# Pairs of PSUM banks as single tiles, in a fused attention and highway kernel

## The chip, the cores and the metric

The kernel runs on one core of a Trainium2 chip. The metric is device time in microseconds (us) of one launch; lower is better. The profile is one execution, and its span runs from the first to the last instruction, about 1.8 us less than the device time.

The granted TensorE clock (1.0 is full speed) differs between executions. Single runs of one kernel differ by 1 to 2 us. All ratios and verdicts below use the runs that were classed as fast. The medians in the tables are of all runs: those of e1, e3, e11 and e12 each contain one run classed as slow.

## The reference

Inputs are q, k and v of shape (8, 8, 576, 64), two 512x512 weights and a bias.

```python
q_s = exp(q - max(q, -1));  q_s /= sum(q_s, -1)          # over the 64 columns
k_s = exp(k - max(k, 2));   k_s /= sum(k_s, 2)           # over the 576 tokens
kv  = einsum('bhsd,bhse->bhde', k_s, v)                  # 64x64 per head
x   = einsum('bhsd,bhde->bhse', q_s, kv)  ->  (4608, 512)
H = relu(x @ w_h);  T = sigmoid(x @ w_t + b_t)
out = T * H + (1 - T) * x
```

## The kernel before

There are eight rounds of attention, b = 0 to 7, one per batch. Each exponentiates q and k, transposes q on TensorE (`q_trans`, three groups of transposes, profile name `pq`), forms the kv products (`kv_half`, `psk`), divides them by the sums that a column of ones has gathered (`kv_norm`), and multiplies out x (`x_pair`, `px`, for eight of nine token blocks; `x_left`, `px_l`, for the ninth). Beside round b + 1 run the dense products of chunk c = b: gate (`pt`) and carry (`ph`), then `nat` tiles that turn the result back for output. The program is emitted in a hand-made order of "slots", eight per round, and each engine gets its part in that order; TensorE's list from 9.81 to 22.11 us keeps it, group by group. The program holds eight banks of PSUM; before the change four serve gate and carry, three rotate for attention, one turns results back.

```python
    ps_ht = pool("ps_ht", 4, space=PSUM)
    ps_q = pool("ps_q", 3, space=PSUM)
    ps_nat = pool("ps_nat", 1, space=PSUM)
    # ... cut ...
    def warm_mid(n):                       # matmuls on zeros
        t = ps_q.tile([P, 512], FP32, tag="qx", name="warm_mid")
        for _ in range(n):
            mm(t, ident, wide, True, True)
    # ... cut ...
    def kv_norm(b):
        rz = small.tile([P, 2, 2], FP32, tag="rz", name=f"rz_{b}")
        for x in range(2):
            nc.vector.reciprocal(rz[:, x], psk[b][x][:, :, 64])
        for x in range(2):
            nc.vector.tensor_mul(kvn[b % 2][:, x], psk[b][x][:, :, 0:64],
                                 rz[:, x].broadcast_to([P, 2, 64]))
    # ... cut ...
    def x_pair(b, a, even=False, home=None):
        # ... cut: two one-bank tiles t[0], t[1]; four 64x64 matmuls of 512 columns ...
        for c in range(2):
            dst = xT[g][:, 2 * a + c, :, b2, :]
            if (c == 0) if even else (b > 2 or a + c < 2):
                nc.scalar.copy(dst, t[c])
            else:
                nc.vector.tensor_copy(dst, t[c])
```

The softmax here doesn't subtract the row's maximum and nothing guards it: scores larger than these inputs give would overflow.

Of the kernel before, what the change touches and what calls it, by code (L numbers as in the profile page):

```python
# [9 lines left out]
FP32 = mybir.dt.float32  # L10
FP16 = mybir.dt.float16
# [3 lines left out]
PSUM = bass.MemoryType.PSUM  # L15
# [3 lines left out]
def kernel(  # L19
# [10 lines left out]
    nc = tc.nc  # L30
    B, H, S, D = q.shape
    P = 128
    PAD = 128
    N9 = S // 64
    NM = N9 - 1
# [4 lines left out]
    def heads_view(t, b):  # L40
        return t[b].rearrange("(c x) (p n) d -> (x p) c (n d)", x=2, n=N9)

    pool = lambda name, bufs, **kw: ctx.enter_context(tc.tile_pool(name=name, bufs=bufs, **kw))
# [10 lines left out]
    gp = pool("gp", 2)  # L54
    mo = pool("mo", 3)
    ps_ht = pool("ps_ht", 4, space=PSUM)
    ps_q = pool("ps_q", 3, space=PSUM)
    ps_nat = pool("ps_nat", 1, space=PSUM)

    ctx.enter_context(tc.manual_schedule())  # L60
# [2 lines left out]
        o, l, r, start=st, stop=sp, skip_group_check=True  # L63
# [90 lines left out]
        for _ in range(n):  # L154
            mm(warm, ident, wide, True, True)

    def warm_mid(n):
        t = ps_q.tile([P, 512], FP32, tag="qx", name="warm_mid")
        for _ in range(n):
            mm(t, ident, wide, True, True)  # L160


    ek, eq, psk, qsT = {}, {}, {}, {}
# [28 lines left out]

    def kv_half(b, a):
        if a == 0:
            psk[b] = [
                ps_q.tile([P, 2, 256], FP32, tag="qx", name=f"psk_{b}_{x}")
                for x in range(2)
            ]
        for n in range(N9):
            for c in range(2):  # L200
                for x in range(2):
                    r = slice(64 * x, 64 * x + 64)
                    mm(
                        psk[b][x][64 * c : 64 * c + 64, a, 0:65],
                        ek[b][r, n, 2 * a + c, :], v16s[b % 2][r, n, 2 * a + c, 0:65],
                        n == 0, n == N9 - 1,
                    )

    def kv_norm(b):
        rz = small.tile([P, 2, 2], FP32, tag="rz", name=f"rz_{b}")  # L210
        for x in range(2):
            nc.vector.reciprocal(rz[:, x], psk[b][x][:, :, 64])
        for x in range(2):
            nc.vector.tensor_mul(
                kvn[b % 2][:, x], psk[b][x][:, :, 0:64],
                rz[:, x].broadcast_to([P, 2, 64]),
            )

    qsum = {}

# [33 lines left out]
        e, r = eq[b][:, n0:n1], qsum[b][:, n0:n1]  # L254
        nc.gpsimd.tensor_mul(e, e, r.broadcast_to(list(e.shape)))  # L255

    def q_trans(b, g, eng=None):
        if g == 0:
            qsT[b] = qtp.tile([P, 4, N9, 64], FP16, tag="qsT", name=f"qsT_{b}")
        n0, n1 = NG[g]  # L260
        w = n1 - n0
        t = ps_q.tile([P, 4, 4, 64], FP16, tag="qx", name=f"pq_{b}_{g}")
        for n in range(n0, n1):
            for a in range(2):
                ptrans(
                    t[:, 2 * a : 2 * a + 2, n - n0, :],
                    eq[b][:, n, 2 * a : 2 * a + 2, :].rearrange("p c d -> p (c d)"),
                )
        if eng is nc.scalar:
            nc.scalar.copy(qsT[b][:, :, n0:n1, :], t[:, :, 0:w, :])  # L270
        else:
            nc.vector.tensor_copy(qsT[b][:, :, n0:n1, :], t[:, :, 0:w, :])  # L272

    def x_pair(b, a, even=False, home=None):
        ps, tag = home or (ps_q, "qx")
        g, b2 = b // 2, b % 2
        if a == 0 and b2 == 0:
            xT[g] = xtp.tile([P, 4, NM, 2, 64], FP16, tag="xT", name=f"xT_{g}")
        t = [
            ps.tile([P, NM, 64], FP32, tag=tag, name=f"px_{b}_{a}_{c}")  # L280
            for c in range(2)
        ]
        for x in range(2):
            for c in range(2):
                r = slice(64 * c, 64 * c + 64)
                mm(
                    t[c][64 * x : 64 * x + 64].rearrange("p n d -> p (n d)"),
                    kvn[b % 2][r, x, a, :],
                    qsT[b][r, 2 * a + x, 0:NM, :].rearrange("p n d -> p (n d)"),
                    True, True,  # L290
                )
        for c in range(2):
            dst = xT[g][:, 2 * a + c, :, b2, :]
            if (c == 0) if even else (b > 2 or a + c < 2):
                nc.scalar.copy(dst, t[c])  # L295
            else:
                nc.vector.tensor_copy(dst, t[c])

    def x_left(b):
        for c in range(2):  # L300
            t = ps_q.tile([P, 2, 64], FP32, tag="qx", name=f"px_{b}_l{c}")
            r = slice(64 * c, 64 * c + 64)
            for a in range(2):
                for x in range(2):
                    mm(
                        t[64 * x : 64 * x + 64, a, :], kvn[b % 2][r, x, a, :],
                        qsT[b][r, 2 * a + x, NM, :], True, True,
                    )
            x9v = x9.rearrange("p (a c) b d -> p a c b d", c=2)
            nc.vector.tensor_copy(x9v[:, :, c, b, :], t)  # L310


    rows_of = lambda c: 8 if c < B else 4
# [9 lines left out]

    live = {}

    def gate(c, ob, home=None):
        xv = views(c)[0]
        ps, tag = home or (ps_ht, "ht")
        ps = ps.tile([P, rows_of(c), 64], FP32, tag=tag, name=f"pt_{c}_{ob}")
        for k_ in range(4):  # L330
            mm(ps, w16["t"][:, k_, ob * P : ob * P + P], xv(k_), k_ == 0, k_ == 3)
        nc.scalar.activation(ps, ps, AF.Tanh, bias=bt2[:, ob : ob + 1], scale=0.5)  # L332
        live[c, ob] = ps
# [36 lines left out]
    o32 = {}  # L370
# [11 lines left out]
    def out_tile(g, n, spare=False):  # L382
        if n % 4 == 0:
            o32[g, n // 4] = og.tile([P, 4, 512], FP32, tag="o32", name=f"o32_{g}_{n}")
        ps, tag = (ps_q, "qx") if spare and n % 4 < 3 else (ps_nat, "nat")
        t = ps.tile([P, 4, P], FP32, tag=tag, name=f"nat_{g}_{n}")
        for k_ in range(4):
            turn_block(
                t, k_,
                None if k_ in added(g) else xT[g][:, k_, n].rearrange("p b d -> p (b d)"),  # L390
                gT[g][:, k_, n].rearrange("p b d -> p (b d)"),
            )
        o = o32[g, n // 4][:, n % 4, :]
        if spare and n % 2:
            nc.vector.tensor_copy(o, flat(t))
        else:
            nc.scalar.copy(o, flat(t))  # L397
        if n % 4 == 3:
            i = n // 4
            nc.sync.dma_start(rows[g][:, 4 * i : 4 * i + 4, :], o32[g, i])  # L400
# [8 lines left out]
    def tile9(g, nk):  # L409
        if g % 2 == 0:  # L410
            o32["9", g // 2] = og.tile([P, 4, 512], FP32, tag="o32", name=f"o9_{g}")
        t = ps_q.tile([P, 4, P], FP32, tag="qx", name=f"nat9_{g}")
        for k_ in range(nk):
            turn_block(t, k_, blk9(x9, g, k_), blk9(g9, g, k_))
        o = o32["9", g // 2][:, g % 2, 0 : nk * P]
        if g % 2:
            nc.vector.tensor_copy(o, flat(t)[:, 0 : nk * P])
        else:
            nc.scalar.copy(o, flat(t)[:, 0 : nk * P])
        if g % 2:  # L420
            nc.sync.dma_start(
                rows9[:, g - 1 : g + 1, 0 : nk * P],
                o32["9", g // 2][:, 0:2, 0 : nk * P],
            )
# [13 lines left out]
    def at(p, *fs):  # L438
        events.setdefault(p, []).extend(fs)
# [37 lines left out]
    for b in range(2, B):  # L477
        p = 8 * (b - 1)
        if b > 2:
# [11 lines left out]
            at(s + 0.9, E(cast_v, b, 1))  # L491
            at(s + 1, E(exp_half, b, "k", 1))
        tr, kv, x = {
            2: ((5, 6, 6.4), (4, 6.2), (7, 7.5, 7.6)),
            3: ((4, 5, 5), (3, 4), (6, 7, 7)),
            4: ((2, 3, 4), (4, 5), (6, 7, 7)),
        }.get(b, ((2, 3, 4), (3, 4), (5, 6, 7)))
        for i in range(3):
            at(p + tr[i], E(q_trans, b, i))
        at(p + kv[0], E(kv_half, b, 0))  # L500
        at(p + kv[1], E(kv_half, b, 1), E(kv_norm, b))
        at(p + x[0], E(x_pair, b, 0))
        at(p + x[1], E(x_pair, b, 1))
        at(p + x[2], E(x_left, b))
    for b in range(4, B):
        at(8 * (b - 3), *[E(load, b, w) for w in "qkv"])

    for f in [
# [3 lines left out]
        E(q_recip, 0), E(q_scale_v, 0, 0, 4), E(q_scale_v, 0, 4, N9),  # L512
        E(exp_half, 0, "k", 0), E(cast_v, 0, 0),
        E(exp_half, 0, "k", 1), E(cast_v, 0, 1),
        E(q_trans, 0, 0), E(q_trans, 0, 1), E(warm_up, 2), E(q_trans, 0, 2),
        E(warm_up, 6),
        E(kv_half, 0, 0), E(gate_bias), E(warm_up, 2), E(kv_half, 0, 1), E(kv_norm, 0),
        *[E(cast_weight, "t", k_, (nc.vector, nc.gpsimd)[k_ % 2]) for k_ in range(4)],
        E(warm_up, 4),
        E(x_pair, 0, 0), E(warm_up, 2), E(x_pair, 0, 1), E(warm_up, 1), E(x_left, 0),  # L520
        E(exp_half, 1, "q", 0), E(q_sums_tree, 1, 0),
        E(exp_half, 1, "q", 1), E(q_sums_tree, 1, 1), E(q_recip, 1),
        *[f for k_ in range(4) for f in (E(less_one, k_), E(cast_weight, "h", k_, nc.scalar, 0.5))],
        E(q_scale_p, 1, 0, 4), E(q_scale_p, 1, 4, 8),
        E(gate, 0, 0), E(gate, 0, 1), E(gate, 0, 2, (ps_q, "qx")), E(warm_mid, 5),
        E(carry, 0, 0), E(blend, 0, 0), E(carry, 0, 1), E(exp_half, 1, "k", 0),
        E(gate, 0, 3, (ps_nat, "nat")), E(blend, 0, 1), E(carry, 0, 2),
        E(q_trans, 1, 0), E(blend, 0, 2), E(carry_products, 0, 3),
        E(exp_half, 1, "k", 1),
        *[E(cast_v_head, 1, c, (nc.scalar, nc.gpsimd, nc.gpsimd, nc.scalar)[c]) for c in range(4)],  # L530
# [2 lines left out]
        *[E(load, 3, w) for w in "qkv"],  # L533
        E(q_trans, 1, 1), E(kv_half, 1, 0), E(kv_half, 1, 1), E(kv_norm, 1),
        E(q_trans, 1, 2), E(carry_diff, 0, 3), E(exp_half, 2, "q", 0),
        E(x_pair, 1, 0, True), E(x_pair, 1, 1, True, (ps_ht, "ht")),
        E(q_sums_tree, 2, 0), E(exp_half, 2, "q", 1), E(q_sums_tree, 2, 1), E(q_recip, 2),
    ]:
        f()
# [33 lines left out]
```

## Time and profile before

| | before |
|---|---|
| device time, median of the first three runs | 132.56 us (132.47 to 132.88) |
| span of the profiled run | 130.5 us, mean clock 0.996 |
| TensorE busy | 115.9 us (89 %) |
| VectorE busy | 101.0 us, 204 instructions |
| ScalarE busy | 93.0 us, 140 instructions |

Two views carry the argument: the table of busy time by windows, and the list of instructions in order of time, with start, duration, engine, line, operation and count, and the idle time before an instruction and what ended it in square brackets. The prediction below shows and reads both.

### The profile page before, as it was taken

What the parts mean: (1) busy time and instruction counts of PE and PEld (TensorE: products, weight loads), DVE (VectorE), ACT (ScalarE), POOL (GpSimd) and SP (SyncE); (2) the same over time, 40 slices, a digit from 0 to 9 for tenths busy, and PEclk for the clock granted to TensorE, in tenths of its full rate; (3) what the DMA queues carried; (4) which work ended last, traced back from release to release, by engine and by line L of the source; (5) the groups of instructions that cost most, each with busy time, mean ns of one, the idle gap of its engine ahead of it and who ended that gap; (6) DMA issues with size and microseconds to landing.
All of it is one profiled execution on the core that took longest, in us unless ns stands there. A gap on an engine that the chain in (4) does not pass through costs nothing.

```text
span 130.5 us, 3496 instructions
## 1 busy us (share of the span) xinstructions
PE 115.9 (89%) x1427; PEld 65.4 (50%) x1427; DVE 101.0 (77%) x204; ACT 93.0 (71%) x140; POOL 69.8 (53%) x64
## 2 busy tenths in 40 slices
PE   4969998996998799789998999989998999999960
PEld 1325442362444246536644654565466445589940
DVE  1397546898999997996996789987986756689870
ACT  3552049997988589669979969968992674666530
POOL 2005506690399999459919970996299523510000
PEclk9999999999999999999999999999999999999998
DMA  4999999999999999998999989990034006037874
GB/s 130 365 384 396 402 400 412 410 413 413 402 412 402 410 413 410 404 411 353 321 379 409 368 285 407 407 403 15 0 158 171 0 5 294 28 161 316 362 290 165
DMA packets 15848, 40.07 MB, mean 307 GB/s; under 512 B 724, under 2 KB 1240, under 8 KB 14808
## 3 DMA queue, kind: packets, MB, share of 16 engines
q1 hardware_dynamic: 15832, 39.85, 79.1%
q8 instruction: 11, 0.18, 0.5%
q14 instruction: 5, 0.04, 0.1%
HBM read 30.41 MB, written 9.44 MB: 305 GB/s over the span
## 4 chain that ended last, share of the span: by engine, by line
PE 43%; DVE 21%; DMA 11%; ACT 8%; issue 6%; POOL 5%; SPq 3%; DVEq 0%; POOLq 0%; ACTq 0%
PE pt L62 14%; PE ph L62 13%; DMA q<-in_q_dram 11%; PE nat L62 6%; DVE r L225 5%; DVE dd L350 4%; PE psk L62 4%; POOL eq L255 3%; PE pq L67 3%; DVE g L358 3%; PE px L62 2%; DVE qsT L272 2%; SPq L94 2%; ACT xT L295 2%; POOL v L182 2%
## 5 line engine op out<-in xcount | busy, mean ns | idle before, releaser
L255 POOL TENSOR_TENSOR eq<-eq,r 128x1024 f16<-128x1024 f16 (+2 forms) x16 | 29.7, 1874 | 15.9 <-DVE r L243 15.9
L332 ACT ACTIVATE pt<-pt,bt 128x512 f32<-128x512 f32 (+1 forms) x40 | 24.8, 624 | 14.1 <-PE pt L62 14.1
L62 PE MATMUL ph<-xT,w16h 128*128 128x512 f16 x128 | 33.3, 380 | 0.8 <-ACT w16h L114 0.4
L62 PE MATMUL pt<-xT,w16t 128*128 128x512 f16 x128 | 32.7, 380 | 1.2 <-ACT xT L295 0.9
L350 DVE SCALAR_TENSOR_TENSOR dd<-xT,ph 128x512 f16<-128x512 f16 x32 | 21.8, 682 | 7.8 <-PE ph L62 6.7
L358 DVE SCALAR_TENSOR_TENSOR g<-pt,dd 128x512 f16<-128x512 f32 (+1 forms) x40 | 25.0, 627 | 2.4
L367 POOL TENSOR_TENSOR g<-g,xT 128x512 f16<-128x512 f16 x18 | 20.4, 1152 | 8.1 <-DVE g L358 8.1
L170 ACT ACTIVATE eq<-q 128x1152 f16<-128x1152 f32 x16 | 18.6, 1176 | 5.8 <-DMA q<-in_q_dram 5.8
L62 PEld LDWEIGHTS <-w16t 128*128 128x128 f16 x160 | 14.1, 98 | 14.0 <-issue 2.7
L295 ACT CAST xT<-px 128x512 f16<-128x512 f32 x28 | 15.2, 594 | 8.2 <-PE px L62 8.2
L62 PEld LDWEIGHTS <-w16h 128*128 128x128 f16 x160 | 13.7, 98 | 12.0 <-ACT w16h L114 2.2
L170 ACT ACTIVATE ek<-k 128x1152 f16<-128x1152 f32 x16 | 18.6, 1178 | 1.4 <-DMA k<-in_k_dram 1.4
L225 DVE TENSOR_REDUCE r<-eq 128x18 f32<-128x1152 f16 x12 | 16.1, 1345 | 3.8 <-ACT eq L170 3.8
L182 POOL CAST v<-v 128x1152 f16<-128x1152 f32 x12 | 13.5, 1146 | 9.7 <-DMA v<-in_v_dram 9.7
L397 ACT COPY o<-nat 128x512 f32<-128x512 f32 x28 | 16.9, 603 | 1.9 <-PE nat L62 0.9
L62 PE MATMUL nat<-ident,g 128*128 128x128 f16 x142 | 17.6, 219 | 0.2
L62 PEld LDWEIGHTS <-g 128*128 128x128 f16 x144 | 13.7, 98 | 6.6 <-DVE g L358 0.9
L272 DVE COPY qsT<-pq 128x1024 f16<-128x1024 f16 (+1 forms) x24 | 13.1, 553 | 3.4 <-PE pq L67 3.0
L67 PE MATMUL pq<-ident,eq 128*128 128x128 f16 x144 | 11.8, 219 | 2.1 <-DVE r L249 1.2
L62 PE MATMUL warm<-wide,ident 128*128 128x512 f16 x37 | 11.5, 455 | 1.8 <-DVE wide L151 1.8
L67 PEld LDWEIGHTS <-eq 128*128 128x128 f16 x144 | 9.3, 98 | 5.3 <-ACT ek L170 1.6
L62 PEld LDWEIGHTS <-kvn 64*64 64x64 f16 x128 | 4.2, 104 | 11.2 <-issue 7.5
(49 smaller groups left out, 106.3 us busy)
## 6 DMA issues: line engine op xcount, KB each, us to landing
out_dram<-o SPq DMA_DIRECT2D x8, 1024.0 KB, 5.2
q<-in_q_dram SPq DMA_DIRECT2D x7, 1152.0 KB, 13.8
k<-in_k_dram SPq DMA_DIRECT2D x7, 1152.0 KB, 13.2
v<-in_v_dram SPq DMA_DIRECT2D x5, 1152.0 KB, 13.6
v<-in_v_dram SPq DMA_DIRECT2D x6, 576.0 KB, 11.6
q<-in_q_dram SPq DMA_DIRECT2D x2, 576.0 KB, 4.0
k<-in_k_dram SPq DMA_DIRECT2D x2, 576.0 KB, 6.7
w32t<-in_moe_w_t_dram SPq DMA_DIRECT2D x1, 1024.0 KB, 10.7
```

What stands on the lines that cost most here:

```text
L62: mm = lambda o, l, r, st, sp: nc.tensor.matmul(o, l, r, start=st, stop=sp, skip_group_check=True)
L67: nc.tensor.matmul(o, i, ident, is_transpose=True, start=True, stop=True, skip_group_check=True,)
L170: nc.scalar.activation(dst[b][:, :, 2 * a : 2 * a + 2, :], in32[which][b][:, 2 * a : 2 * a + 2].rearrange("p c n d -> p n c d"), AF.Exp,)
L182: (eng or nc.gpsimd).tensor_copy(o, i)
L225: nc.vector.reduce_sum(qsum[b][:, :, h], eq[b][:, :, h, :], axis=AX.X)
L255: nc.gpsimd.tensor_mul(e, e, r.broadcast_to(list(e.shape)))
L295: nc.scalar.copy(dst, t[c])
L332: nc.scalar.activation(ps, ps, AF.Tanh, bias=bt2[:, ob : ob + 1], scale=0.5)
L350: nc.vector.scalar_tensor_tensor(dd, xv(ob), -0.5, ps, op0=ALU.mult, op1=ALU.max)
L358: nc.vector.scalar_tensor_tensor(gv(ob), th, 1.0, dd, op0=ALU.add, op1=ALU.mult)
L367: nc.gpsimd.tensor_add(gv(ob), gv(ob), xv(ob))
L397: nc.scalar.copy(o, flat(t))
```

## The change

The intent was fewer and larger operations: the kv products and each pair of x tiles sit in one tile of two banks, so that one reciprocal, one multiply and one copy serve both halves; the ninth tokens' small matmuls run beside the pairs; both kv halves share one visit to the 64x64 mode.

```diff
-    ps_q = pool("ps_q", 3, space=PSUM)
+    ps_2 = pool("ps_2", 1, space=PSUM)      # one tile of two banks
+    ps_1 = pool("ps_1", 1, space=PSUM)      # one bank
...
+    def two_banks(name, dt=FP32):
+        return ps_2.tile([P, 2, 2048 // (4 if dt is FP32 else 2)], dt, tag="q2", name=name)
...
-        for x in range(2):
-            nc.vector.reciprocal(rz[:, x], psk[b][x][:, :, 64])
-        for x in range(2):
-            nc.vector.tensor_mul(...)
+        nc.vector.reciprocal(rz, psk[b][:, :, :, 64])
+        nc.vector.tensor_mul(
+            kvn[b % 2], psk[b][:, :, :, 0:64], rz.broadcast_to([P, 2, 2, 64])
+        )
...
+    def x_pair(b, a, how, left=False, singles=False):     # cut to its core
+        if singles: t = two one-bank tiles of ps_ht
+        else:       t = the halves of two_banks(...)
+        # ninth-token matmuls into a ps_1 tile, half with each pair, where left
+        if len(how) == 1: one copy of 1024 columns, by ScalarE ("A")
+        else:             one copy per half, engines by letter ("AV", "AA")
...
-        E(q_trans, 0, 0), E(q_trans, 0, 1), E(warm_up, 2), E(q_trans, 0, 2),
+        E(q_trans, 0, 0), E(q_trans, 0, 1, lambda: held("q0", FP16)[:, 0]), E(warm_up, 2), E(q_trans, 0, 2, lambda: held("q0", FP16)[:, 1]),
...
-        E(x_pair, 0, 0), E(warm_up, 2), E(x_pair, 0, 1), E(warm_up, 1), E(x_left, 0),
+        E(x_pair, 0, 0, "AA"), E(warm_up, 2), E(x_pair, 0, 1, "AV"), E(warm_up, 1), E(x_left, 0),
...
-        E(gate, 0, 2, (ps_q, "qx")), E(warm_mid, 5),
+        E(gate, 0, 2, lambda: held("m0")[:, 0]), E(warm_mid, 5, lambda: held("m0")[:, 1]),
...
     # out_tile and tile9, in the tail
-        ps, tag = (ps_q, "qx") if spare and n % 4 < 3 else (ps_nat, "nat")
+        if spare and n % 4 < 2: t = half n % 4 of one two_banks tile
+        else: ps, tag = (ps_1, "q1") if spare and n % 4 == 2 else (ps_nat, "nat")
...
-            3: ((4, 5, 5), (3, 4), (6, 7, 7)),
-            4: ((2, 3, 4), (4, 5), (6, 7, 7)),
-        }.get(b, ((2, 3, 4), (3, 4), (5, 6, 7)))
+            3: ((4, 5, 5), (4, 4), (6, 7)),
+            4: ((2, 3, 4), (5, 5), (6, 7)),
+        }.get(b, ((2, 3, 4), (4, 4), (5, 6)))
```

The last lines are the slots of transposes, kv halves and x pairs of a round. `held("m0")` gives gate 0,2 one half of a two-bank tile and the warm-up matmuls the other; `held("q0")` does the same with the second and third group of round 0's transposes.

## The prediction

> **What bounds the kernel now.** I call the eight rounds of attention b = 0 to 7; the program orders work in slots, eight per round, one gate or carry product (four matmuls of 512 columns) per slot. I read the page first: busy share per engine, then the chain that ended last, then the busy time by windows.
>
> ```profile
> PE 43%; DVE 21%; DMA 11%; ACT 8%; issue 6%; POOL 5%; SPq 3%; DVEq 0%; POOLq 0%; ACTq 0%
> ```
> ```profile
> 30.00:41.00 11.00, 9.29 (x127) 4.55 (x130) 10.52 (x24) 10.25 (x14) 6.27 (x6) 1.00 1.04 409
> 41.00:50.00 9.00, 7.73 (x114) 3.65 (x101) 8.73 (x18) 6.37 (x10) 8.74 (x8) 1.00 1.04 408
> 50.00:60.00 10.00, 8.72 (x112) 5.14 (x111) 8.32 (x18) 7.82 (x13) 6.71 (x5) 1.00 1.03 403
> 70.00:80.00 10.00, 10.00 (x150) 5.85 (x148) 7.76 (x16) 8.96 (x14) 7.36 (x6) 1.00 0.99 355
> 90.00:100.00 10.00, 9.63 (x115) 5.40 (x114) 9.45 (x16) 8.04 (x13) 6.51 (x5) 1.00 0.26 107
> 100.00:113.00 13.00, 13.00 (x133) 6.87 (x132) 7.89 (x18) 7.95 (x15) 5.79 (x6) 1.00 0.20 83
> ```
> Columns are window, length, PE, PE loads, DVE, ACT, POOL, clock, DMA. Up to about 30 us input DMA and start-up rule; from 30 to 41 DVE has almost no gap (10.52 of 11.00); from 60 to 123 PE is full, apart from 0.37 us holes. So an instruction saved on DVE or ACT pays only from 30 to 55 us, and later only PE time pays. PE's order in time shows what it does between the dense products (b = 6 to b = 7, with its unhidden waits):
>
> ```profile
> 96.80 0.61 PE L67 MATMUL pq<-ident,eq 128*128 128x128 f16 x8
> 97.45 0.69 DVE L272 COPY qsT<-pq 128x1024 f16<-128x1024 f16 x1 [0.16 <-PE pq L67]
> 98.11 0.61 PE L67 MATMUL pq<-ident,eq 128*128 128x128 f16 x8
> 99.09 0.48 PE L62 MATMUL psk<-v,ek 64*64 64x65 f16 x36 [0.37 <-POOL v L182]
> 99.50 1.04 PE L62 MATMUL pt<-xT,w16t 128*128 128x512 f16 x4
> ...
> 92.20 1.04 PE L62 MATMUL ph<-xT,w16h 128*128 128x512 f16 x4
> 93.16 0.43 PE L62 MATMUL px_l<-qsT,kvn 64*64 64x64 f16 x8
> 93.53 1.04 PE L62 MATMUL pt<-xT,w16t 128*128 128x512 f16 x4
> ```
> Starts are what to read, as ends are modelled. Between dense products four matmuls take 0.865 us from start to start (59.62 back to 58.76 gives 0.86). Before a group of 64*64 matmuls it is 0.96 (92.20 to 93.16): entering small tiles costs about 0.09. The px_l visit costs 0.37 + 0.09 = 0.46 in all.
>
> [...] ACT copies of 128, 384 and 512 columns take 266, 480 and 587 ns, hence 0.836 ns per column and 159 ns fixed. But neighbours overlap: two xT casts of 594 ns take 1.07 us together, not 1.19.
>
> **The change, part by part.**
> 1. Norm in two ops, not four. Before: two reciprocals 0.23 us and two multiplies 0.46 in the chain, 0.69. After: one reciprocal 0.12, one multiply of 256 columns; from 286 ns at 128 columns and about 1.07 ns per DVE column (dd 682 at 512, 410 at 256) 423 ns, about 0.37 net of overlap. Saves 0.20 of DVE per round.
> 2. One x copy per pair on ACT: 159 + 1024 x 0.836 = 1.015 us against 1.07. Saves 0.05, but the first half comes no earlier than the second.
> 3. One ninth-token copy instead of two: about 0.34 against 0.40 of DVE (94.64 to 95.04). Saves 0.06.
> 4. Both kv halves in one visit for b = 3 to 7: one entry less, 0.09, and some of the exit: 0.15 of PE. For b = 6 and 7 the first half also comes a slot later, so the 0.37 wait for POOL's v cast should vanish.
> 5. Ninth-token matmuls beside the pairs: for b = 5 to 7 the px_l visit disappears, 0.46 less two times 0.13 for four matmuls inside the pairs: 0.2 of PE.
> 6. Buffers: three rotating banks become one tile of two banks and one single bank. Each transpose group must now await the copy of the one before. At 96.80 to 98.14 the copy ends just where the next group starts: about 0.08 per round for b = 4 to 7. It is worse in b = 3, where groups two and three are adjacent in one slot:
>
> ```profile
> 52.35 0.72 PE L67 MATMUL pq<-ident,eq 128*128 128x128 f16 x10
> 52.91 1.03 PE L62 MATMUL pt<-xT,w16t 128*128 128x512 f16 x4
> 53.64 0.68 DVE L350 SCALAR_TENSOR_TENSOR dd<-xT,ph 128x512 f16<-128x512 f16 x1
> 54.23 0.88 DVE L272 COPY qsT<-pq 128x1024 f16<-128x1024 f16 x2
> 54.97 0.41 PE L62 MATMUL px<-qsT,kvn 64*64 64x512 f16 x4 [0.70 <-DVE qsT L272]
> ...
> 56.73 1.07 ACT L295 CAST xT<-px 128x512 f16<-128x512 f32 x2 [0.24 <-PE px L62]
> 57.37 0.25 PE L62 MATMUL px_l<-qsT,kvn 64*64 64x64 f16 x4 [0.58 <-ACT xT L295]
> ```
> All ten transposes went at once and PE did a gate product while DVE was behind. Now the last two wait for the copy that DVE reaches only at 54.2, and gate, turn-back (1.2 us) and pair come after. The second pair also waits for the first pair's single copy (1.02 us against 0.97 + 0.34 between their starts), and the next gate, one slot on, for the second copy.
>
> **The sum.** Up to b = 2: DVE loses 0.20 + 0.06 on its path, -0.25. b = 2: its second pair moves to other banks; the waits of 0.47 and 0.34 before px and px_l shrink, -0.4. b = 3: I walked the order with the durations above. Norm ends near 51.7, sums and dd to 53.5, copy two to 54.15, last transposes 54.3, gate and turn-back to 55.5, pair one to 56.05, carry to 57.0, pair two awaits the copy to 57.2, its own copy runs to 58.6, and the gate's last two blocks wait for that: PE reaches the turn-back at 59.1, before 58.43. So +0.67 for b = 2 and 3 together (b = 2's -0.4 included). b = 4: ACT starts the first copy at 67.9 as before, pair two waits to 69.0 (before 68.38), the gate for a copy ending 70.4: +0.25. b = 5: -0.15 - 0.2 + 0.08, about -0.3. b = 6 and 7: the same and -0.37, -0.65 each. From there PE sets the end, so all passes through: -0.25 + 0.67 + 0.25 - 0.3 - 1.3 = -0.93. Predicted 132.56 - 0.93, **131.6 us**.
>
> **The rivals.** (a) The loop through DVE and POOL becomes the bound: kv product, norm, sums, two POOL scalings (4.19 us), two v casts (2.24 us), next kv product. For: PE's two 0.37 holes come from it. Against: only the second half had to await the second cast, which ended at 100.1 and was used at 100.9. I get 11.2 us per round for this loop, 11.4 for PE, 12.08 now. If it binds, about 0.6 is lost: 132.2. (b) The single buffers cost more than the visits give: pair two waiting on ACT in every round, or the copies late because DVE is late. For: ACT's first copy in b = 6 starts at 90.66, only after an exponential. Against: it would end near 91.7, pair two began at 91.86. Then the time is 133 to 134. (c) The b = 3 stall doesn't appear, because DVE catches up earlier with fewer ops, and gains stay whole: 130.3 or less. (d) Everything saved lies off the path: 132.5.
>
> **Range and chances.** The gains are near 2.6 us (0.25 + 0.4 + 1.9), the losses near 1.7, and both are estimates from starts; an error of a third on each is about 1 us. Range 130.3 to 132.9. Two per cent are 2.65 us: faster needs all gains and no loss, 0.07; slower needs about 3.6 us of new waits beyond my sum, 0.03; within two per cent 0.90.
>
> **What would show it.** Right: a PE wait of more than 1 us for the qsT copy in b = 3; px waiting for ACT in b = 3 and 4 and the gate after it too; no wait for POOL v in b = 6 and 7; rounds 5 to 7 nearer 11.4 than 12.08 us; norm near 0.5 us; one xT copy near 1.02 us. Wrong if the two-bank ops carry a cost of their own, if pairs of b = 5 to 7 wait for ACT, if psk waits for POOL as before, or if another release of banks makes the gates wait.

Two points of the walk were the author's estimate. One is that TensorE holds what is emitted behind a waiting transpose; it was measured afterwards in the changed kernel, where the transposes that waited 1.80 us start at 58.99 and the gate behind them at 59.10 us. The other is part 4's 0.15 us: the entry of 0.09 is read from the trace, the rest is not.

## More of the kernel before

```profile
17.10 0.69 DVE L297 CAST xT<-px 128x512 f16<-128x512 f32 x1 [0.46 <-PE px L62]
17.88 2.76 PE L62 MATMUL pt<-xT,w16t 128*128 128x512 f16 x12
...
20.48 1.24 PE L62 MATMUL warm_mid<-wide,ident 128*128 128x512 f16 x5
...
22.11 2.81 PE L62 MATMUL ph<-xT,w16h 128*128 128x512 f16 x8 [0.39 <-ACT w16h L114]
```

Three gates of chunk 0 run from 17.88, five warm-up matmuls on zeros keep TensorE occupied from 20.48, and the first carry products begin at 22.11, as soon as ScalarE has cast the carry weights.

## The result

The changed kernel took 136.89 us as a median of four runs (136.56 to 138.31), the kernel before 132.52 us. The ratio is 1.0342, with a 95 % interval of 1.0277 to 1.0407. Ratios here are the mean time of one kernel's fast runs over the mean of the other's in the same rounds, so they are not quite the ratio of the medians. The change makes the kernel slower by 3.4 %; the prediction had 131.6 us and gave a slowdown of over 2 % a chance of 0.03.

The profiled run of the changed kernel has a span of 136.5 us at a mean clock of 0.967. First, its chain of waits by engine:

```profile
PE 61%; DVE 18%; ACT 11%; DMA 3%; issue 3%; SPq 0%; DVEq 0%; ACTq 0%
```

DMA's share of the chain fell from 11 to 3 % and ScalarE's rose from 8 to 11 %. Before, the chain passed through the landing of round 1's q at 19.3 us; now it passes through round 0's own work, TensorE and the x copies, from 6 us on. The table by windows, for two of the windows that the prediction shows:

```profile
30.00:41.00 11.00, 8.87 (x132) 4.37 (x131) 9.96 (x22) 8.99 (x13) 1.73 (x3) 1.00 1.04 410
100.00:113.00 13.00, 12.96 (x175) 7.29 (x173) 9.50 (x18) 8.54 (x14) 8.56 (x7) 1.00 0.22 89
```

VectorE is no longer gapless between 30 and 41 us (9.96 of 11.00), and late in the run TensorE is as full as before (12.96 of 13.00), so the loss lies elsewhere. Stage by stage, from the start of the first carry product of each chunk in the two profiles:

| first carry product of chunk | before, us | changed, us | difference | change of the interval |
|---|---|---|---|---|
| 0 | 22.11 | 27.46 | +5.35 | |
| 1 | 33.22 | 37.82 | +4.60 | start: +4.60 |
| 2 | 45.89 | 50.02 | +4.13 | -0.47 |
| 3 | 58.76 | 64.58 | +5.82 | +1.69 |
| 4 | 71.02 | 76.95 | +5.93 | +0.11 |
| 5 | 82.66 | 88.33 | +5.67 | -0.26 |
| 6 | 94.74 | 99.68 | +4.94 | -0.73 |
| 7 | 106.82 | 111.03 | +4.21 | -0.73 |
| end of the span | 130.5 | 136.5 | +6.0 | tail: +1.8 |

The interval that ends at chunk c holds round c of attention. Rounds 5 to 7 gained 1.72 us, close to the 1.6 that was predicted. Round 3 lost more than predicted, and the start and the tail lost 4.60 and 1.8 us, where the prediction had -0.25 and nothing.

**The start.** The list in order of time for the changed kernel:

```profile
19.12 0.41 PE L63 MATMUL px<-qsT,kvn 64*64 64x512 f16 x4 [0.64 <-ACT xT L336]
...
19.57 0.59 ACT L336 CAST xT<-px 128x512 f16<-128x512 f32 x1 [0.51 <-PE px L63]
...
20.19 0.69 DVE L336 CAST xT<-px 128x512 f16<-128x512 f32 x1 [2.16 <-ACT xT L336]
...
20.94 0.26 PE L63 MATMUL px_l<-qsT,kvn 64*64 64x64 f16 x8 [1.09 <-DVE xT L336]
...
21.13 3.06 PE L63 MATMUL pt<-xT,w16t 128*128 128x512 f16 x8
...
23.98 1.60 PE L63 MATMUL m<-xT,w16t 128*128 128x512 f16 x4
...
25.67 0.66 ACT L362 ACTIVATE m<-m,bt 128x512 f32<-128x512 f32 x1 [0.19 <-ACT pt L362]
...
26.38 1.24 PE L63 MATMUL m<-wide,ident 128*128 128x512 f16 x5 [0.80 <-ACT m L362]
...
27.46 1.89 PE L63 MATMUL ph<-xT,w16h 128*128 128x512 f16 x8
```

Three things are new. VectorE's copy of one half of a pair waits for ScalarE's copy of the other half (20.19 after 19.57 + 0.59), though they read different banks. The warm-up matmuls at 26.38, named `m` because they write a half of gate 0,2's tile, wait for ScalarE's tanh on the other half (0.80 us), and the carry products behind them in TensorE's order start only at 27.46, though ScalarE had cast their weights by 24.35 us (22.18 + 2.17). And the eight gate matmuls from 21.13 to 23.98 take 0.36 us each, where the kernel before took 2.60/12 = 0.22: the clock had dropped after the idle time. The table by windows for TensorE alone shows that (window, length, busy time, clock, DMA share, GB/s):

```profile
19.00:22.00 3.00, 1.80 (x17) 0.95 1.05 405
22.00:25.00 3.00, 3.00 (x9) 0.50 1.04 410
```

The longest single gap of TensorE between 17.5 and 22 us is 1.09 us; what came before the drop is several short gaps in a row, with 1.80 of 3.00 us busy from 19 to 22.

The waits of the first two kinds are in the program and are not only inferred from the trace. The compiled instruction lists of the two kernels, with the engine whose semaphore each instruction waits for (DVE is VectorE, Activation is ScalarE):

```
before   Matmult warm_mid<-wide,ident                   [waits DVE]
changed  Matmult m0, second half<-wide,ident            [waits Activation]
before   TensorCopy xT<-px_0_1_1 (VectorE)              [waits PE]
changed  TensorCopy xT<-px_0_1, second half (VectorE)   [waits Activation]
before   Matmult pq_0_2<-ident,eq                       [waits for nothing]
changed  Matmult q0, second half<-ident,eq              [waits DVE]
```

The last two lines are a wait of the same kind that comes still earlier: the last two transposes of round 0 wait for VectorE's copy of the other half of `q0`. It is seen best in the trace of e4 (below), whose start is that of the changed kernel and whose clock is full until 16 us:

```profile
12.06 0.27 PE L68 MATMUL q<-ident,eq 128*128 128x128 f16 x2 [0.35 <-DVE qsT L278]
```

The first transposes start at the same time there as in the kernel before (9.79 and 9.81 us), these at 12.06 and not at 11.56, and the first kv product at 13.55 and not at 13.06. No run below removes this wait.

**Round 3 and the tail**, from the list in order of time of TensorE:

```profile
56.58 0.61 PE L68 MATMUL pq<-ident,eq 128*128 128x128 f16 x8
58.99 0.27 PE L68 MATMUL pq<-ident,eq 128*128 128x128 f16 x2 [1.80 <-DVE qsT L278]
...
63.82 0.59 PE L63 MATMUL pt<-xT,w16t 128*128 128x512 f16 x2 [0.51 <-ACT xT L333]
...
128.42 0.22 PE L63 MATMUL nat<-ident,x 128*128 128x128 f16 x1 [0.28 <-ACT o L455]
```

Round 3 shows the two predicted waits: 1.80 us for the transposes' bank, 0.51 for the late half of an x copy. In the tail, the second of two output tiles that share a two-bank tile waits for ScalarE's copy of the first. There are four such waits on TensorE (0.28 us three times, and 0.61), 1.45 us in sum; the kernel before has none of them.

### The profile page after: what moved, and what is told of

It reads as the page before. It is cut to its first block, busy times and chain, and to the rows that moved or that the text cites. A ratio compares the mean times of both kernels' runs of the same rounds, so it can differ in the third digit from the quotient of the medians.

```text
span 136.5 us, 3464 instructions
## 1 busy us (share of the span) xinstructions
PE 116.0 (85%) x1427; PEld 65.0 (48%) x1427; DVE 99.3 (73%) x180; ACT 92.6 (68%) x129; POOL 69.5 (51%) x64
## 4 chain that ended last, share of the span: by engine, by line
PE 61%; DVE 18%; ACT 11%; DMA 3%; issue 3%; SPq 0%; DVEq 0%; ACTq 0%
PE pt L63 18%; PE ph L63 17%; PE nat L63 8%; PE pq L68 5%; DVE dd L380 4%; PE psk L63 4%; ACT xT L333 4%; DMA q<-in_q_dram 3%; PE warm L63 3%; DVE g L388 3%; PE px L63 3%; ACT o L432 2%; DVE r L230 2%; DVE qsT L278 2%; ACT xT L336 2%
## 5 line engine op out<-in xcount | busy, mean ns | idle before, releaser
L63 PE MATMUL pt<-xT,w16t 128*128 128x512 f16 x124 | 34.0, 390 | 2.4 <-ACT xT L333 1.0
L362 ACT ACTIVATE pt<-pt,bt 128x512 f32<-128x512 f32 (+1 forms) x39 | 24.1, 621 | 16.9 <-PE pt L63 16.9
L63 PE MATMUL ph<-xT,w16h 128*128 128x512 f16 x128 | 32.8, 380 | 0.0
L388 DVE SCALAR_TENSOR_TENSOR g<-pt,dd 128x512 f16<-128x512 f32 (+1 forms) x39 | 24.4, 627 | 2.7
L63 PEld LDWEIGHTS <-w16t 128*128 128x128 f16 x160 | 14.9, 100 | 18.0 <-issue 7.5
L68 PE MATMUL pq<-ident,eq 128*128 128x128 f16 x134 | 11.1, 219 | 5.1 <-DVE qsT L278 2.7
L333 ACT CAST xT<-px 128x1024 f16<-128x1024 f32 x11 | 11.2, 1016 | 4.4 <-PE px L63 3.4
L63 PE MATMUL warm<-wide,ident 128*128 128x512 f16 x37 | 12.1, 472 | 1.8 <-DVE wide L152 1.8
L278 DVE COPY qsT<-pq 128x1024 f16<-128x1024 f16 (+1 forms) x22 | 12.3, 561 | 1.2 <-PE pq L68 0.6
L63 PE MATMUL nat<-ident,xT 128*128 128x128 f16 x56 | 9.7, 219 | 0.0
```

The lines of the kernel that those rows point to most:

```text
L63: mm = lambda o, l, r, st, sp: nc.tensor.matmul(o, l, r, start=st, stop=sp, skip_group_check=True)
L68: nc.tensor.matmul(o, i, ident, is_transpose=True, start=True, stop=True, skip_group_check=True,)
L278: nc.vector.tensor_copy(qsT[b][:, :, n0:n1, :], t[:, :, 0:w, :])
L333: copy[how](dst, t2.rearrange("p c (n d) -> p c n d", d=64))
L362: nc.scalar.activation(ps, ps, AF.Tanh, bias=bt2[:, ob : ob + 1], scale=0.5)
L388: nc.vector.scalar_tensor_tensor(gv(ob), th, 1.0, dd, op0=ALU.add, op1=ALU.mult)
```

## The experiments

The theory after the first look, T: inside a two-bank tile the program orders all accesses of different engines as if they touched the same bank. Where the kernel put unrelated things into the halves (a gate and the warm-ups; two output tiles) or gave the halves to two engines, that makes waits at the start and in the tail, and the idle time at the start lowers the clock as well (0.50 from 22 to 25 us, after the three us with 1.80 busy). I call such an order, which no data needs, a false order. Rivals: C, the clock alone, which differs between executions; X, only the waits of round 0's x pairs matter; H, the tail is hidden behind the output transfers.

All outputs are right. Each is compared with runs of the kernel before on the same chip.

| run | median, us | ratio to before | 95 % interval |
|---|---|---|---|
| a0, changed kernel again | 137.41 | 1.0364 | 1.0291 to 1.0437 |
| e1, warm-ups moved | 135.51 | 1.0211 | 1.0135 to 1.0288 |
| e3, round 0's pair moved | 139.10 | 1.0472 | 1.0392 to 1.0551 |
| e4, tail tiles apart | 135.20 | 1.0232 | 1.0169 to 1.0296 |
| e5, all three | 132.91 | 1.0054 | 1.0022 to 1.0086 |
| e6, e5 and round 3's transposes | 131.07 | 0.9909 | 0.9874 to 0.9944 |
| e7, e6 and two ops for late copies | 131.13 | 0.9907 | 0.9873 to 0.9941 |
| e8, e5 with the single ops undone | 132.90 | 1.0047 | 1.0019 to 1.0074 |
| e9, e6 and round 2's ninth tokens later | 131.08 | 0.9884 | 0.9836 to 0.9932 |
| e10, e9 and one copy in round 1 | 130.11 | 0.9832 | 0.9781 to 0.9883 |
| e11, e6 with two kv visits | 132.39 | 0.9996 | 0.9940 to 1.0051 |
| e12, e6 with ninth tokens apart | 133.03 | 1.0034 | 0.9985 to 1.0083 |

### a0: the changed kernel again

No edit.

> The changed kernel again, unaltered, for more runs and another profile. Theory T (false orders inside two-bank tiles: warm-up matmuls wait for a gate's tanh, halves of the tail wait for each other): about 136.6 us whenever the granted clock is 0.995 as in the kernel before, and up to 138.3 when it is lower. Rival C (the loss is the throttled TensorE clock of the start, 0.967 in the first profile): time follows the clock and comes near 132.5 us where the clock is 0.995.

Its four fast runs were 138.16, 136.79, 138.03 and 136.73 us at clocks 0.967, 0.994, 0.982 and 0.995. At 0.994 and 0.995 it is still 4.4 to 5.0 us slower than the kernel before, whose four runs on that chip at 0.993 to 1.0 took 131.79 to 132.37 us. So the clock's difference between executions explains some 1.4 us of a single run, not the loss: rival C falls as the sole cause.

### e1, e3 and e4: one false order at a time

e1 lets the warm-ups write the single bank:

```diff
-        E(warm_mid, 5, lambda: held("m0")[:, 1]),
+        E(warm_mid, 5, lambda: ps_1.tile([P, 512], FP32, tag="q1", name="warm_mid")),
```

> One edit: the five warm-up matmuls after gate 0,2 write the single bank and not the other half of the gate's two-bank tile. Theory T: their 0.8 us wait for the tanh of gate 0,2 is gone, and the first carry products start near 23 us and not 27.5 us; time 132.5 to 133.5 us, 3 to 4 us less than the changed kernel. Rival C (clock): no change beyond 0.5 us. Rival X (the waits of round 0's second pair and ninth tokens, 0.64 and 1.09 us, carry the loss): no change beyond 0.5 us, since these remain.

e3 gives round 0's second pair two banks of its own:

```diff
-        E(x_pair, 0, 1, "AV"),
+        E(x_pair, 0, 1, "AV", False, True),     # singles: two ps_ht banks
```

> One edit: round 0's second x pair goes into two single gate banks and not into the two-bank tile. Theory T: the first gate matmul of round 0 starts 1 to 1.7 us earlier (before 20 us), but the warm-up matmuls still wait for the tanh of gate 0,2, which ScalarE reaches at its own time, so the whole stays within 0.5 us of the changed kernel. Rival X: 1 to 1.7 us faster.

e4 uses only the first half of the two-bank tile in the tail, in rotation with the two single banks:

```diff
-        if spare and n % 4 < 2:
-            if n % 4 == 0:
-                o32["2"] = two_banks(f"nat_{g}_{n}")
-            t = o32["2"][:, n % 4].rearrange("p (k d) -> p k d", k=4)
+        if spare and n % 3 == 0:
+            t = two_banks(f"nat_{g}_{n}")[:, 0].rearrange("p (k d) -> p k d", k=4)
         else:
-            ps, tag = (ps_1, "q1") if spare and n % 4 == 2 else (ps_nat, "nat")
+            ps, tag = (ps_1, "q1") if spare and n % 3 == 1 else (ps_nat, "nat")
     # and tile9 likewise: ps_2's first half and ps_1 in turn
```

> One edit: in the last eight output tiles and the ninth-token tiles only the first half of the two-bank tile is used, rotating with the two single banks, so no two tiles share a tile object. Theory T: the four waits of 0.28 us each on ScalarE's copy vanish and the copies of neighbours run side by side; from the last full gate (118.1 us in the profile) to the end 16.6 us now as in the kernel before and not 18.4; 1.2 to 1.8 us faster than the changed kernel. Rival H (the tail is hidden behind the last output transfers): within 0.3 us of the changed kernel.

e1 gained 1.5 % on a0, about half of what T had expected, and e3 lost 1 %, though the intervals of e3 and a0 overlap. Neither number fits T or X as they were written. The trace of e3 tells why. TensorE's list in order of time, then TensorE's windows:

```profile
25.72 2.29 PE L63 MATMUL m<-wide,ident 128*128 128x512 f16 x5 [3.78 <-ACT m L362]
```
```profile
25.00:28.00 3.00, 2.28 (x6) 0.52 1.05 413
```

Gate 0,2 starts at 20.91, 3 us earlier than the 23.98 of the changed kernel, as expected, but the warm-ups still await the tanh, now for 3.78 us, and after that gap the clock is at half: the five warm-ups take 0.42 us each. Being early only lengthened the idle time. In e1 the warm-ups are free, but the idle time of the x pairs is left, and the twelve gate matmuls take 0.36 us each, from 21.13 to 25.42 (its profile fell in a slow run). So two things that were each right in part hold the same stretch, and removing one leaves it to the other.

e4 behaved as T had it: from the first gate of the ninth chunk to the end it takes 133.2 - 116.56 = 16.6 us, as the kernel before (130.5 - 113.87 = 16.6), where the changed kernel took 136.5 - 118.08 = 18.4. The ratio fell from 1.0364 to 1.0232, which is 1.7 us. The tail's loss follows the shared tile, and rival H falls.

### e5: the three together

> Three edits together: warm-ups into the single bank, round 0's second pair into two gate banks, tail tiles not sharing a tile. The first three runs suggest that the start needs both edits, since each alone leaves one wait that idles TensorE and lowers its clock (pt matmuls took twice as long after the idle). Theory T with that addition: first gate at about 19.2 us, first carry product at about 23 us and not 27.5, clock 0.985 or more, 130 to 131.3 us: faster than the kernel before, since rounds 5 to 7 keep their gain. Rival P (each edit adds only its own: -1.9 and -1.8 and nothing or +1.5): 133 to 135 us.

The pt matmuls that "took twice as long" are seen in the changed kernel: their weight loads lie 0.43 us apart between 21.85 and 24.83 us, where four matmuls take 0.865 at a clock of 1.00.

Its edit is those of e1, e3 and e4. TensorE's list in order of time and its windows:

```profile
18.27 1.90 PE L63 MATMUL pt<-xT,w16t 128*128 128x512 f16 x8
...
21.94 2.06 PE L63 MATMUL ph<-xT,w16h 128*128 128x512 f16 x8
```
```profile
22.00:25.00 3.00, 3.00 (x15) 1.00 1.05 412
```

The first carry product starts at 21.94, against 22.11 before and 27.46 in the changed kernel, and the clock stays at 1.00. The ratio went from 1.0232 (e4) to 1.0054: the two start edits together are worth 1.8 %, about 2.4 us, and all three 3.1 %, about 4.1 us. The times alone do not exclude rival P: with e3's edit counted as nothing, the gains of e1 and e4 add up to a ratio of 1.0079, inside e5's interval (with e3's loss counted, to 1.0187, outside it). The traces decide. The time from the first kv product to the first carry product leaves out what happened to the clock before:

| trace | first kv product, us | first carry product, us | between them |
|---|---|---|---|
| before | 13.06 | 22.11 | 9.05 |
| changed | 15.05 | 27.46 | 12.41 |
| e4, start unaltered | 13.55 | 25.95 | 12.40 |
| e1, warm-ups moved | 15.06 | 26.50 | 11.44 |
| e3, pair moved | 14.92 | 27.80 | 12.88 |
| e5, both | 14.01 | 21.94 | 7.93 |

Alone, one edit gains 0.97 us in this stretch and the other loses 0.47; together they gain 4.48. So the start needs both, as T says, and not P. Two false orders remain in e5 and in the runs built on it: that of the `q0` transposes, and that of round 1's first pair, which ScalarE and VectorE copy one after the other (e10 removes it). The time itself, 132.91 us, is 1.6 to 2.9 us above the range expected for this run: I had counted the gain of rounds 5 to 7 and too little of round 3's loss. In this profile the chunks start at 33.18, 45.88, 60.44, 72.80, 84.18, 95.53 and 106.88: level with the kernel before at chunk 2, 1.68 us behind at chunk 3, level again at chunk 7 (106.82 before). The 0.47 us that round 2 seemed to gain in the changed kernel is not there (12.70 against 12.67 before).

### e6: round 3's transposes

```diff
-            at(p + tr[i], E(q_trans, b, i))
+            home = (lambda: two_banks("pq_3_2", FP16)[:, 0]) if (b, i) == (3, 2) else None
+            at(p + tr[i], E(q_trans, b, i, home))
```

> As the run with three edits, and round 3's last two transposes go into the two-bank tile, free since the norm, and not behind the copy of the eight before. Theory T: TensorE's 1.80 us wait for the qsT copy in round 3 falls to under 0.4, some 0.3 to 0.8 of it comes back as a wait of the first pair for that copy; 0.8 to 1.5 us faster than the run with three edits. Rival Q (VectorE is the bound there and TensorE would wait for it at the next place anyway): within 0.4 us.

The ratio fell from 1.0054 to 0.9909, which is 1.9 us and more than the 0.8 to 1.5 expected. All ten transposes go at once again, and the wait comes back in part before the pair:

```profile
52.74 0.72 PE L68 MATMUL pq<-ident,eq 128*128 128x128 f16 x10
...
55.35 0.22 PE L63 MATMUL px_l<-qsT,kvn 64*64 64x64 f16 x2 [0.69 <-DVE qsT L279]
```

From chunk 1 to chunk 3 it takes 26.11 us, where e5 takes 27.26 and the kernel before 25.54. By the traces the edit is thus worth 1.15 us; what the remaining 0.7 us of the ratio come from I could not tell (the granted clocks of the runs overlap). This version, 0.6 to 1.3 % faster than the kernel before by its interval, shows that the schedule's gain exists once the false orders that cost the most and this wait are gone.

### e7: late copies in halves

```diff
-        at(p + x[1], E(x_pair, b, 1, "AV" if b == 2 else "A", b > 2, b == 2))
+        at(p + x[1], E(x_pair, b, 1, {2: "AV", 3: "AA", 4: "AA"}.get(b, "A"), b > 2, b == 2))
```

> As the run before it in this list, and the second pairs of rounds 3 and 4 are copied in two ScalarE ops of 512 columns, not in one of 1024. Theory T: the next gate's third matmul waits for half a copy; its two waits of 0.51 us fall to about 0.1, 0.4 to 0.9 us faster. Rival S (two ops take longer in sum, so the fourth matmul waits instead): within 0.3 us.

The ratio is 0.9907 against 0.9909, within 0.3 us, as rival S had it. By the traces the intervals that end at chunks 3 and 4 are 12.88 and 12.21 us, against 13.04 and 12.36 in e6: 0.3 us in sum, too little for the comparison to show. ScalarE needs about as long for two copies of 512 columns (1.07 us together, before) as for one of 1024 (1.016, changed), and the gate needs the last block in any case.

### e8: the single ops undone

```diff
-        nc.vector.reciprocal(rz, psk[b][:, :, :, 64])
-        nc.vector.tensor_mul(kvn[b % 2], psk[b][:, :, :, 0:64], ...)
+        for x in range(2): nc.vector.reciprocal(rz[:, x], psk[b][:, x, :, 64])
+        for x in range(2): nc.vector.tensor_mul(kvn[b % 2][:, x], psk[b][:, x, :, 0:64], ...)
...
-        at(p + x[0], E(x_pair, b, 0, "A", b > 2))
+        at(p + x[0], E(x_pair, b, 0, "AA", b > 2))     # the second pair likewise
```

> As the run with three edits, but with the single ops undone: norm in four VectorE ops and each x copy in two ScalarE ops, on the same two-bank tiles. Theory T: the merging of ops itself is worth little, since TensorE bounds rounds 3 to 7: the same within 0.5 us, at most 0.7 slower. Rival O (the merged ops carry the gain): 1.5 us or more slower than the run with three edits.

Its ratio is 1.0047, against 1.0054 for e5: the merged norm and x copies, the first half of the change's purpose, are worth nothing that can be measured here, and rival O falls. (The merged ninth-token copy stayed as it was; it was not tested.) The changed kernel has 24 VectorE instructions fewer than the kernel before, and 1.7 us less VectorE work (99.3 against 101.0), but off the path.

### e9 and e10: more of the same kind

e9 moves round 2's `x_left` behind the next gate, since it waited 0.9 us for ScalarE's copy; e10 also copies round 1's first pair by one ScalarE operation.

```diff
-            at(p + 7.6, E(x_left, 2))
+            at(p + 8.5, E(x_left, 2))
# e10 only
-        E(x_pair, 1, 0, "AV"),
+        E(x_pair, 1, 0, "A"),
```

> As the run with four edits (three edits and round 3's last transposes moved), and round 2's ninth tokens come one slot later, after the next gate. Theory T: TensorE's 0.9 us wait of px_l for ScalarE's copy vanishes, an entry into small tiles of 0.09 us is added; 0.4 to 0.8 us faster than the run with four edits, near 130.4. Rival D (VectorE, nearly gapless from 30 to 50 us, sets the pace there): within 0.2 us.

> As the run before it in this list, and round 1's first pair is copied by one ScalarE op and not by ScalarE and then, one after the other because both halves are one tile, VectorE. Theory D (VectorE-bound there): 0.69 us of VectorE falls away, 0.3 to 0.7 us faster. Rival A (ScalarE, busy with exponentials there, becomes late): same or slower.

e9's ratio, 0.9884, is not told apart from e6's 0.9909. Its trace shows where the 0.9 us went:

```profile
45.08 1.07 PE L63 MATMUL pt<-xT,w16t 128*128 128x512 f16 x4 [0.91 <-DVE dd L381]
```

The gate now waits as long for VectorE, which is behind there: rival D. e10 has 0.9832, its six runs average 130.50 us against 130.97 for e9; that is the direction of theory D, but the runs overlap, so I leave it open. With a median of 130.11 us, e10 is the fastest version measured, 1.2 to 2.2 % faster than the kernel before.

### e11 and e12: the schedule's two gains alone

Both undo one part of the change in rounds 5 to 7 only.

```diff
# e11: kv halves a slot apart
-        }.get(b, ((2, 3, 4), (4, 4), (5, 6)))
+        }.get(b, ((2, 3, 4), (3, 4), (5, 6)))
# e12: ninth tokens in their own visit
-        at(p + x[0], E(x_pair, b, 0, "A", b > 2))
+        at(p + x[0], E(x_pair, b, 0, "A", 2 < b < 5))  # and x[1] likewise
+        if b > 4:
+            at(p + 7, E(x_left, b))
```

> As the run with four edits, but in rounds 5 to 7 the two kv halves go back to two visits, a slot apart. Theory T (prediction's part 4): the wait for POOL's v cast of some 0.4 us returns in rounds 6 and 7 and each round has one more entry into small tiles of 0.09 us: rounds of 11.35 us become 11.5 to 12.0, 0.6 to 1.5 us slower in all. Rival: within 0.3 us.

> As the run with four edits, but in rounds 5 to 7 the ninth tokens get their own visit in slot 7 again. Theory T (prediction's part 5): each round gains 0.46 and loses 0.26 to 0.3 us of TensorE: 0.4 to 0.7 us slower in all. Rival: within 0.3 us.

e11 has 0.9996 where e6 has 0.9909, 1.2 us. The two ran on different chips and their intervals just touch, but the traces agree: from chunk 4 to chunk 7 it takes 35.65 us in e11 and 34.08 in e6. The old wait is back:

```profile
99.19 0.48 PE L63 MATMUL psk<-v,ek 64*64 64x65 f16 x36 [0.41 <-POOL v L194]
```

The interval from chunk 6 to chunk 7 is 106.76 - 94.72 = 12.04 us there, against 11.35 with one visit. e12 has 1.0034, 1.7 us above e6 (35.82 us from chunk 4 to chunk 7), more than the 0.4 to 0.7 expected:

```profile
94.06 0.26 PE L63 MATMUL px_l<-qsT,kvn 64*64 64x64 f16 x8 [0.53 <-ACT xT L334]
```

The separate visit must use the two-bank tile and waits 0.53 us for the pair's copy in each round, so it measures the placement together with this wait. Its interval is 107.40 - 95.47 = 11.93 us.

## Why the prediction was wrong

- **The start was the step that failed.** In "The sum" the prediction put "Up to b = 2: DVE loses 0.20 + 0.06 on its path, -0.25", and its first paragraph set the first 30 us down to input DMA and start-up. The profile showed +4.60 us at chunk 1 at a clock of 0.967, and the run e4, whose start is unaltered, +3.09 (36.31 against 33.22) at 0.986. In its place stand the false orders of the two-bank tiles, and the clock that drops after the idle time they make (0.50 from 22 to 25 us in the first profile, 0.72 from 19 to 22 in e4). e5 removes the two largest of them and has chunk 1 at 33.18.
- **The tail was counted as nothing.** It lost 1.8 us, and with the tiles apart (e4) this loss is gone.
- Behind both stands an assumption that part 6, on the buffers, never stated: that the halves of a two-bank tile are independent because they are different banks. The program list shows that they are not. Part 6 looked for waits on a bank's release only. The warm-ups' new place and the output tiles' are plain in the diff; they were read as harmless.
- **Round 3: right mechanism, wrong size.** Rounds 2 and 3 were to lose 0.67 us together and lost 1.22, and in e5, where the start is as before, 1.72. The 1.80 us wait for the copy and the 0.51 wait of the gate came as described. Two terms were mis-sized: round 2's -0.4 isn't there in e5 (12.70 us against 12.67), and round 3's +1.07 is +1.69 (14.56 against 12.87).
- **Rounds 4 to 7 were right.** Predicted +0.25, -0.3, -0.65, -0.65; measured +0.11, -0.26, -0.73, -0.73. TensorE's period was put at 11.4 us and is 11.35. Two kv halves in one visit take 0.71 us from start to next start (93.63 to 94.34), against two times 0.41 before: 0.11 less, besides the one entry of 0.09; part 4 had put both at 0.15. The v-cast waits are gone, and e11 brings them back. Rival (a), the loop through POOL, did not bind.
- **The merged ops: the copies were sized right, the norm was not.** The copy of 1024 columns takes 1.016 us (1.015 predicted). The norm takes 0.18 and 0.42 us; from its start to the next VectorE operation it is 0.56 us (34.20 to 34.76, round 1) against 0.61 before (29.72 to 30.33), so it saves 0.05 us a round and not the 0.20 of part 1. Part 1 took the old norm from its start to its end and the new one net of overlap. e8 shows no effect of these ops on the time. The prediction's -0.25 for them does not show at chunk 1 of e5 either (33.18, before 33.22), but the two false orders that e5 keeps lie before it.
- **The sum.** At chunk 7 e5 is level with the kernel before (+0.06 us), where the prediction has -0.93. Of the difference, rounds 2 and 3 are 1.05 us and the missing -0.25 is 0.21; rounds 4 to 7 were 0.26 better than predicted. The predicted 131.6 us is a ratio of 0.993. That it lies between e5 (1.0054) and e6 (0.9909) is chance, as the prediction has neither e5's loss in round 3 nor e6's cure for it.

How the first profile's 5.35 us at the first carry product divide can be read from the starts. Before the first kv product lie 1.99 us; 1.20 of these are in the six warm-up matmuls that end there (2.59 us against 1.39), at a clock of 0.68 to 0.75. From the first x pair to the first gate it takes 3.60 us against 2.34: 1.26, the waits of the pairs. The three gates take 4.45 us against 2.60: 1.85, the lowered clock. The last 0.25 us lie at the second warm-ups. These shares do not add up to what each edit would save, as e1 and e3 show.

The 1.20 us need not come from the change. In the five traces whose windows were read, the clock between 10 and 13 us goes with TensorE's idle time before round 0's first transposes: it is 0.75 and 0.74 in the changed kernel and e3, with 2.35 and 2.14 us of idle time, and 1.00 in the kernel before, e4 and e5, with 1.18, 1.12 and 1.39. In a0 and e1, with 2.18 and 2.50, the six warm-ups took 2.68 and 2.40 us from start to next start; in e6, with 1.64, they took 1.38. What stays open is why this idle time differs between executions of the same start, and where e6's last 0.7 us come from.

## What to carry to other kernels

Before joining buffers into one tile, list what shares it and which engine touches each half: the ordering here went by the tile that the program names (VectorE's read of one half began at 20.19 us, when ScalarE's of the other had ended at 20.16), so halves with different users became a queue. The merged operations paid nothing here (e8, 1.0047 against 1.0054), off the path. Read the start and the tail of a schedule as closely as the steady state, and check filler work such as warm-up matmuls: here five that waited 3.78 us (e3) held the carry products behind them until 27.80 us. When two edits each seem to do little or harm, try them together if they act on the same stretch.
